# Scale arithmetic from VectorE to GpSimd, a dependency between the last two half products, and another order list

## The chip, the cores and the metric

The kernel runs on one core of a Trainium2 chip. The time is the device time in microseconds (us) of one execution, the median of several runs. The engines are PE (TensorE, matrix products, with its weight loads as PEld), DVE (VectorE), ACT (ScalarE), POOL (GpSimd) and SP, which issues the transfers here. Each engine runs its own list of instructions in order and waits on semaphores for the others.

## The reference

`x` is 4 x 8 x 512 x 64 and `state` 4 x 8 x 32 x 64. Attention goes both ways between them, its result is 2176 rows of 512, and two MLPs follow.

```
scores = scale * x @ state^T;  a = softmax(scores)  (sum + 1e-9);  xread = a @ state
scores2 = scale * state @ x^T; a2 = softmax(scores2) (sum + 1e-9); sread = a2 @ x
x = concat([xread, sread], axis=2)  -> rows of H*D = 512, 2176 of them
h = x @ w_in            (512 -> 2048)
g = h * tanh(softplus(h))
x = g @ w_out           (2048 -> 512)
xn = x / sqrt(mean(x*x) + 1e-6) * rms_g
g = xn @ w_gate; val = xn @ w_val       (512 -> 1536)
out = (g * sigmoid(g) * val) @ w_out2   (1536 -> 512)
```

## The kernel before

The rows are worked on in four chunks of 512 (one for each batch) and one of 128 rows for the state reads. A weight matrix is cut in column or row groups of 512, `wi` and `wo` of the first MLP (four groups u each), `wg`, `wv` and `w2` of the second (three each). The first products of the run are full float32 ones (`full_l1` in `full_group`, L978, and `full_l2`, L1002, on PE). Later ones take a weight or an activation as a sum of two float16 parts, high and low, and in the second MLP products of quarters are combined in the manner of Strassen (L1255 for gate and value, L1339 `lprod` for the last layer), so that DVE and ACT have sums of quarters to form.

For the float16 parts each tensor is scaled by a power of two. `pow2` (L398 to L421) finds it: PE sums norms over the partitions (L402), DVE reduces and bounds them (L410, L411 or L413), a shift leaves an exponent `q` (L414), and two integer operations on one column (or four) make of it the scale `s` (L416) and its inverse `si` (L417). `times` and `scalar` (L428 to L441, the instruction is L439) form products of such scales, and `bounds` (L873 to L886, L876, L881, L882) products, minima and maxima of them. They live in columns of small tiles named `page`. `split` (L543 to L556) then writes the scaled high part (`sh`, through `copy_to`, L385 to L392, on ACT at L388 or on DVE at L390 and L392) and the low part (`sl`, DVE, L550). `fetch` (L456 to L520) loads a weight and joins its words: `hi` (L388 or L392), `low` (L492 on ACT, L494 on DVE), `sign` (L499 or L503), and the join on DVE (L517).

`attention` (L655 to L830) has for its first heads, in DVE's and ACT's lists: a transpose of the scores (L778), their maxima (L783, L785, L786), the exponentials on ACT (L789), and for the softmax over the state a maximum, a subtraction (L791, L792) and exponentials (L794), totals (L798 to L800), a product (L803) and a transpose back (L805).

`finish` ends a chunk: the last products go to PSUM banks a_89 to a_92, DVE adds them to partial sums (`end add`, L1393), adds what was kept from an earlier pass (`end more`, L1399), and the results leave by transfers on SP's queue. For the last chunk the product A22 T4 is done in two halves, each followed by an add on DVE (L1445).

Nothing is scheduled on the chip. Every piece of work is an `op` with the engines that can take it, a cost in us (the planner's, no measurement), and the names it reads and writes. The order in which ops are emitted is a written-out list of numbers, `SEQ` (L32 to L136): a number halved is the op, and its low bit says that an op which can go to ACT or DVE takes DVE. `Plan.run` walks the list:

```
        for k in SEQ:
            o = self.ops[k >> 1]
            assert o.deps <= done
            done.add(o)
            e = "V" if k & 1 else next(x for x in o.engs if x != "V" or len(o.engs) == 1)
```

The order on each engine is that of the list; waits between engines are put in afterwards, from what the instructions read and write. A PSUM bank that one engine reads is not read by another at the same time, and it is not written while it is still read.

Of the kernel before, what the change touches and what calls it, by code (L numbers as in the profile page):

```python
# [211 lines left out]
def v1(n):  # L212
    return 0.069 + n / 960
# [23 lines left out]
def attn_moe_moe_kernel(  # L237
# [12 lines left out]
    nc = tc.nc  # L250
# [146 lines left out]
    def pow2(part, pnames, k, floor, nm, xexp, most=0, to=None):  # L397
# [10 lines left out]
        def fn(e):  # L408
            if most:
                nc.vector.tensor_reduce(t, P[b][:, :k], AX.X, ALU.max)  # L410
                nc.vector.tensor_scalar(t, t, floor, 2.0 * most, ALU.max, ALU.mult)  # L411
            else:
                nc.vector.tensor_scalar(t, P[b][:, :k], floor, 2.0, ALU.max, ALU.mult)  # L413
# [1365 lines left out]
```

## Time and profile before

| | before |
|---|---|
| median of 3 runs | 708.99 us (708.34 to 709.17) |
| the profiled execution | 707.23 us, of which the span is 705.4 |
| granted clock of PE | 0.999 of full speed |
| busy in the span | PE 691.7, DVE 645.2, ACT 435.5, POOL 0.7 us |

The span reaches from the first to the last instruction that the profiler records. Busy is the time in which an engine had an instruction in work; small instructions on DVE and ACT overlap with their neighbours, so what one of them costs its engine is the distance from its start to the next start, which can be shorter than its duration.

### The profile page before, as it was taken

The numbers are of one execution on the slowest core, as the hardware profiler recorded it, in microseconds if no ns is written. First come the engines' busy times: TensorE is split into PE (matmuls) and PEld (weight loads), VectorE is DVE, ScalarE is ACT, GpSimd is POOL, SyncE is SP. The second block draws the span as 40 slices with busy tenths as digits, with TensorE's granted clock in tenths as the row PEclk, the third lists the DMA queues.
The fourth block names the chain that finished last, engine by engine and source line by source line (L and its number), as shares of the span: only waits on it lengthen the run. The fifth ranks groups of instructions, "written<-read, shape, count | busy, mean of one in ns | idle before, by whom it ended". The sixth has DMA issues, their size and how long they took to land.

```text
span 705.4 us, 14169 instructions
## 1 busy us (share of the span) xinstructions
PE 691.7 (98%) x5818; PEld 491.2 (70%) x5818; DVE 645.2 (91%) x1182; ACT 435.5 (62%) x729; POOL 0.7 (0%) x6
## 2 busy tenths in 40 slices
PE   8899999999999999999999999999999999999996
PEld 6444444444444444476898889988889988898985
DVE  5999999999999999999999999997788687899997
ACT  5999999998896899898956565332122222123330
POOL 0000000000000000000000000000000000000000
PEclk9999999999999999999999999999999999999999
DMA  7786524256245571375810021520056630333225
GB/s 242 222 253 196 206 91 136 89 173 202 76 169 170 211 246 72 129 249 206 288 43 36 25 91 44 194 108 31 16 214 216 213 136 31 120 136 107 88 70 185
DMA packets 42100, 101.05 MB, mean 143 GB/s; under 512 B 16692, under 2 KB 18740, under 8 KB 39604
## 3 DMA queue, kind: packets, MB, share of 16 engines
q1 hardware_dynamic: 42036, 100.15, 41.9%
q8 instruction: 45, 0.74, 0.4%
q14 instruction: 19, 0.16, 0.1%
HBM read 67.90 MB, written 32.24 MB: 142 GB/s over the span
## 4 chain that ended last, share of the span: by engine, by line
PE 75%; DVE 19%; ACT 3%; DMA 2%; issue 1%; SPq 0%; DVEq 0%; ACTq 0%
PE p L1255 28%; PE a L1120 14%; PE a L1339 13%; PE p L1044 6%; PE a L1002 4%; PE p L978 2%; PE p L1486 2%; DVE g L1082 2%; PE p L1052 2%; DVE psm L550 1%; DVE slot L1137 1%; PE a L1533 1%; DVE rms L939 1%; DVE slot L1393 1%; DMA attm<-in_moe_w_gate_dram 1%
## 5 line engine op out<-in xcount | busy, mean ns | idle before, releaser
L1120 PE MATMUL a<-g,w2m 128*128 128x512 f16 (+1 forms) x864 | 164.3, 343 | 0.6 <-DVE g L1082 0.4
L1120 PEld LDWEIGHTS <-w2m 128*128 128x128 f16 x864 | 75.6, 98 | 81.3 <-issue 7.0
L1255 PEld LDWEIGHTS <-attm 128*128 128x128 f16 x1008 | 98.3, 98 | 13.2 <-issue 1.8
L1255 PEld LDWEIGHTS <-w 128*128 128x128 f16 x1008 | 98.5, 98 | 11.4
L1267 DVE TENSOR_TENSOR tt<-p,tt 128x512 f32<-128x512 f32 x120 | 81.7, 686 | 17.1 <-PE p L1255 15.1
L1044 PE MATMUL p<-slot,rms 128*128 128x512 f16 x336 | 78.0, 379 | 0.0
L1255 PE MATMUL p<-slot,w 128*128 128x256 f16 x576 | 68.8, 273 | 0.0
L1255 PE MATMUL p<-slot,attm 128*128 128x256 f16 x576 | 68.6, 273 | 0.0
L388 ACT ACTIVATE w2m<-tt 128x512 f16<-128x512 f32 x34 | 21.0, 623 | 67.2 <-DVE tt L1306 27.1
L1339 PEld LDWEIGHTS <-w2m 128*128 128x128 f16 x576 | 56.3, 98 | 8.5 <-issue 2.0
L1044 PEld LDWEIGHTS <-rms 128*128 128x128 f16 x336 | 32.3, 98 | 40.2 <-issue 2.6
L1291 ACT ACTIVATE tt<-tt,page 128x512 f32<-128x512 f32 x36 | 25.4, 714 | 45.9 <-DVE tt L1267 45.8
L1339 PE MATMUL a<-attm,w2m 128*128 128x256 f16 x384 | 45.5, 273 | 1.6 <-DVE slot L1445 1.6
L1339 PEld LDWEIGHTS <-g 128*128 128x128 f16 x432 | 42.2, 98 | 5.4 <-DVE g L1298 0.6
L1066 ACT ACTIVATE tt<-p,page 128x512 f32<-128x512 f32 x60 | 40.0, 683 | 7.3 <-DVE g L1082 5.8
L1082 DVE SCALAR_TENSOR_TENSOR g<-tt,page,g 128x1024 f16<-128x1024 f32 (+1 forms) x32 | 38.6, 1211 | 0.3
L1298 DVE TENSOR_TENSOR w2m<-tt,w2m 128x512 f16<-128x512 f32 x51 | 34.6, 685 | 2.4 <-ACT w2m L388 2.1
L550 DVE SCALAR_TENSOR_TENSOR psm<-psm,page 128x512 f16<-128x512 f32 x49 | 36.1, 742 | 0.6 <-ACT psm L388 0.2
L388 ACT ACTIVATE psm<-psm,page 128x512 f16<-128x512 f32 (+1 forms) x46 | 32.5, 717 | 6.7 <-DVE psm L550 5.2
L1339 PE MATMUL a<-attm,g 128*128 128x256 f16 x288 | 35.2, 273 | 0.3 <-DVE g L1298 0.3
L1393 DVE SCALAR_TENSOR_TENSOR rms<-a,page,rms 128x512 f32<-128x512 f32 x38 | 28.3, 746 | 7.5 <-PE a L1339 5.9
L1317 DVE TENSOR_TENSOR tt<-tt 128x512 f32<-128x512 f32 x48 | 32.7, 687 | 0.7
(248 smaller groups left out, 1214.1 us busy)
## 6 DMA issues: line engine op xcount, KB each, us to landing
psm<-in_moe_w_out_dram SPq DMA_DIRECT2D x14, 1024.0 KB, 5.0
psm<-in_moe_w_in_dram SPq DMA_DIRECT2D x8, 1024.0 KB, 5.0
psm<-in_moe_w_val_dram SPq DMA_DIRECT2D x6, 1024.0 KB, 5.7
part<-rms SPq DMA_DIRECT2D x24, 256.0 KB, 2.6
psm<-part SPq DMA_DIRECT2D x6, 1024.0 KB
kept_wv<-psm SPq DMA_DIRECT2D x9, 512.0 KB, 4.3
kept_w<-psm SPq DMA_DIRECT2D x9, 512.0 KB, 3.5
attm<-in_moe_w_gate_dram SPq DMA_DIRECT2D x4, 1024.0 KB, 5.7
```

Of the source, the lines that this page charges most:

```text
L388: nc.scalar.activation(o, i, ACTF.Copy, scale=1.0 if scale is None else scale)
L550: op({"V": v1(512) + 0.06}, lambda e: nc.vector.scalar_tensor_tensor(lo, f, s, h, ALU.mult, ALU.subtract), r=[*fn_, *hn, sname], w=ln, nam ...
L1044: nc.tensor.matmul(P[ph], P[folds[u][k]][:, a, f:f + 128], xh[:, k, b, :], start=(k, a, b) == (0, 0, 0), stop=(k, a, b) == (1, 1, 0))
L1066: op({"A": a_ps(512) + 0.1}, lambda e, sp=sp, i=i, ph=ph, ce=ce: nc.scalar.activation(P[sp][:, 512 * i:512 * i + 512], P[ph], ACTF.Mish, s ...
L1082: nc.vector.scalar_tensor_tensor(lo, x, rh, hi, ALU.mult, ALU.subtract)
L1120: nc.tensor.matmul(P[ya[d]][:, :n], part("wo", u, f, a)[:, d * 128:(d + 1) * 128], P[g[0]][:, g[1], b, i * n:(i + 1) * n], start=first and ...
L1255: nc.tensor.matmul(P[to][:, f * 256:f * 256 + 256], part(w, u, j, a)[:, k * 256 + f * 128:k * 256 + f * 128 + 128], h[:, k, b, :], start=b ...
L1267: op({"V": v1(512)}, lambda e: nc.vector.tensor_tensor(P[to], P[bank_], P[a], ALU.add), r=[bank_, a], w=[to], name=f"{w} add")
L1298: op({"V": v1(512)}, lambda e: nc.vector.tensor_tensor(P[g][:, 1, :], P[s], P[g][:, 0, :], ALU.subtract), r=[s], w=[g], name="gl")
L1317: op({"V": v1(512)}, lambda e: nc.vector.tensor_tensor(P[o], P[a], P[b], f), r=[a, b], w=[o], name="gsum")
L1339: nc.tensor.matmul(P[to][:, t * 256:t * 256 + 256], P[g][:, a, o:o + 128], part("w2", u, j, b)[:, f * 256:f * 256 + 256], start=begin and ...
L1393: op({"V": v1(512) + 0.06}, lambda e: nc.vector.scalar_tensor_tensor(o(), two(P[bank_]), osc, a(), ALU.mult, ALU.add), r=[bank_, *an, on_] ...
```

## The change

Three things are changed. The pair `s`, `si` of `pow2` becomes an op of its own on GpSimd, and so do the products of `times` and the operations of `bounds`; 89 instructions leave DVE and stand on GpSimd. `lprod` can be told to come after another op, and the second half of the last product A22 T4 is told to come after the add of its first half. And `SEQ` is another list altogether, one row longer, with another order on every engine and other choices between ACT and DVE. Line numbers of the changed kernel are 1 higher up to `pow2`, 5 higher behind it and 6 higher at the end. In all PE has the same instructions, DVE 1111 where it had 1184, ACT 630 where it had 646, and GpSimd 100 where it had 11. Of the instructions that can stand on either, ACT has 14 fewer of 512 columns and 3 fewer of 1024; DVE has them.

```
--- before.py
+++ after.py
@@ SEQ
-32 0 4 46 62 64 58 60 6 9 10 50 34 53 74 48 70 72 66 68 76 100 82 114 138 96 90 126 154 150 80 140 226 160 162 158 164
+0 2 32 48 60 6 4 62 64 66 9 10 52 55 76 160 162 50 68 70 72 74 78 98 96 80 100 158 136 166 168 194 164 228 234 230 232
...
@@ -411,12 +412,16 @@
                 nc.vector.tensor_scalar(t, t, floor, 2.0 * most, ALU.max, ALU.mult)
             else:
                 nc.vector.tensor_scalar(t, P[b][:, :k], floor, 2.0, ALU.max, ALU.mult)
             nc.vector.tensor_scalar(
                 q, t.bitcast(I32), 24, 23, ALU.logical_shift_right, ALU.logical_shift_left)
-            nc.vector.tensor_scalar(s.bitcast(I32), q, -1, (190 + xexp) << 23, ALU.mult, ALU.add)
-            nc.vector.tensor_scalar(si.bitcast(I32), q, (64 - xexp) << 23, None, ALU.add)
-        op({"V": 0.52 + (0.18 if most else 0.0)}, fn, r=[b], w=[(nm, "s")], name=f"pow2 {nm}")
+        def scales(e):
+            nc.gpsimd.tensor_scalar(s.bitcast(I32), q, -1, (190 + xexp) << 23, ALU.mult, ALU.add)
+            nc.gpsimd.tensor_scalar(si.bitcast(I32), q, (64 - xexp) << 23, None, ALU.add)
+        op({"V": 0.31 + (0.14 if most else 0.0)}, fn, r=[b], w=[(nm, "q")], name=f"pow2 {nm}")
+        op({"G": 0.4}, scales, r=[(nm, "q")], w=[(nm, "s")], name=f"pow2 {nm}")
...
-            op({"V": 0.17}, lambda e: fn(t), r=reads, w=[nm], name=str(nm))
+            op({"G": 0.2}, lambda e: fn(t), r=reads, w=[nm], name=str(nm))
...
-            nc.vector.tensor_scalar(t, a, b, c, ALU.mult, ALU.mult if c is not None else ALU.bypass)
+            nc.gpsimd.tensor_scalar(t, a, b, c, ALU.mult, ALU.mult if c is not None else ALU.bypass)
...
-            scalar(("pr", u), [128, 2], lambda t, u=u: nc.vector.tensor_tensor(
+            scalar(("pr", u), [128, 2], lambda t, u=u: nc.gpsimd.tensor_tensor(
...
-                nc.vector.tensor_tensor(t[:, 0:1], lo, sc["pr", u][:, 0:1], ALU.min)
-                nc.vector.tensor_tensor(t[:, 1:2], hi, sc["pr", u][:, 1:2], ALU.max)
+                nc.gpsimd.tensor_scalar(t[:, 0:1], lo, sc["pr", u][:, 0:1], None, ALU.min)
+                nc.gpsimd.tensor_scalar(t[:, 1:2], hi, sc["pr", u][:, 1:2], None, ALU.max)
...
-    def lprod(to, g, u, j, begin=False, ts=(0, 1)):
+    def lprod(to, g, u, j, begin=False, ts=(0, 1), after=()):
...
-        op({"T": cost}, fn, r=[g, *part_names("w2", u, [j])], w=[to] if len(ts) == 2 else [(to, ts[0])], at=clock[0],
+        op({"T": cost}, fn, r=[g, *part_names("w2", u, [j])], w=[to] if len(ts) == 2 else [(to, ts[0])], at=clock[0], after=after,
...
+            got = []
             for k in range(2):
-                lprod(B_, gs["A22"], u, T4, ts=(k,))
-                op({"V": v1(256) + 0.06}, lambda e, k=k, v=v: nc.vector.scalar_tensor_tensor(
+                lprod(B_, gs["A22"], u, T4, ts=(k,), after=got)
+                got = [op({"V": v1(256) + 0.06}, lambda e, k=k, v=v: nc.vector.scalar_tensor_tensor(
                     v[:, k], two(P[B_])[:, k], osc, two(P[a1])[:, k], ALU.mult, ALU.add),
-                    r=[(B_, k), B_, a1, on_], w=rd[k:k + 1], name="end add")
+                    r=[(B_, k), B_, a1, on_], w=rd[k:k + 1], name="end add")]
```

Three places of the order, on DVE unless another engine is named. First the start, where the heads' scores (PSUM banks a_89 to a_92, two banks for each of two halves of the heads, here called the first and the second head) become exponentials. Before, DVE has:

```order
L783 TENSOR_REDUCE page_104<-a_89 128x1 [waits PE_49]
L783 TENSOR_REDUCE page_104<-a_90 128x1 [waits PE_49]
L785 TENSOR_REDUCE page_69<-page_104 128x1 [waits DVE_49]
L786 TENSOR_SCALAR page_69<-page_69 128x1 [waits DVE_49]
L778 STREAM_TRANSPOSE attm<-a_89 128x256 [waits Activation_49]
L778 STREAM_TRANSPOSE attm<-a_90 128x256 [waits Activation_49]
L791 TENSOR_REDUCE page_104<-attm 128x16 [waits DVE_49]
L778 STREAM_TRANSPOSE attm<-a_91 128x256 [waits PE_49]
L778 STREAM_TRANSPOSE attm<-a_92 128x256 [waits PE_49]
```

After, the same place on DVE reads:

```order
L783 STREAM_TRANSPOSE attm<-a_89 128x256 [waits PE_49]
L783 STREAM_TRANSPOSE attm<-a_90 128x256 [waits PE_49]
L788 TENSOR_REDUCE page_104<-a_89 128x1
L788 TENSOR_REDUCE page_104<-a_90 128x1
L790 TENSOR_REDUCE page_69<-page_104 128x1 [waits DVE_49]
L791 TENSOR_SCALAR page_69<-page_69 128x1 [waits DVE_49]
L796 TENSOR_REDUCE page_104<-attm 128x16
L797 TENSOR_TENSOR attm<-attm,page_104 128x512 [waits DVE_49]
L788 TENSOR_REDUCE page_105<-a_91 128x1 [waits PE_49]
L788 TENSOR_REDUCE page_105<-a_92 128x1 [waits PE_49]
L790 TENSOR_REDUCE page_104<-page_105 128x1 [waits DVE_49]
L791 TENSOR_SCALAR page_104<-page_104 128x1 [waits DVE_49]
```

The next two there are the transposes of a_91 and a_92, each marked as waiting for ACT. So the transposes of the first head have moved ahead of its maxima, and those of the second behind the second head's maxima and its exponentials. On ACT the exponentials of the second head (a_91, a_92) stood behind three conversions of weights:

```order
L789 ACTIVATE attm,page_104<-a_90,page_69 128x256
L388 ACTIVATE w_70<-psm 128x1024 [waits DMAHW4_49]
L499 ACTIVATE sxm<-psm 128x1024
L492 ACTIVATE sxm<-psm 128x1024
L789 ACTIVATE attm,page_105<-a_91,page_104 128x256 [waits DVE_49,PE_49]
```

After, ACT has at that place:

```order
L794 ACTIVATE attm,page_104<-a_90,page_69 128x256
L504 ACTIVATE sxm<-psm 128x1024 [waits DMAHW4_49]
L389 ACTIVATE w_70<-psm 128x1024
L497 ACTIVATE sxm<-psm 128x1024
L497 ACTIVATE xs<-psm 128x1024 [waits DMAHW5_49]
L794 ACTIVATE attm,page_105<-a_91,page_104 128x256 [waits DVE_49,PE_49]
```

A fourth conversion, of the next transfer's words, has moved ahead of the exponentials. The second place is the first `pow2` of a weight on DVE (the scales are in page_69, q is in page_106, the weight in w_70). Before:

```order
L410 TENSOR_REDUCE page_106<-p_85 128x1 [waits PE_49]
L411 TENSOR_SCALAR page_106<-page_106 128x1 [waits DVE_49]
L414 TENSOR_SCALAR page_106<-page_106 128x1 [waits DVE_49]
L416 TENSOR_SCALAR page_69<-page_106 128x1 [waits DVE_49]
L417 TENSOR_SCALAR page_69<-page_106 128x1
L803 TENSOR_TENSOR attm<-attm,page_105 128x512
L392 TENSOR_SCALAR w_70<-w_70,page_69 128x512 [waits DVE_49]
```

After, with the pair gone to GpSimd (L420 and L421 there):

```order
L411 TENSOR_REDUCE page_106<-p_85 128x1 [waits PE_49]
L412 TENSOR_SCALAR page_106<-page_106 128x1 [waits DVE_49]
L416 TENSOR_SCALAR page_106<-page_106 128x1 [waits DVE_49]
L508 TENSOR_SCALAR sxm<-psm 128x1024 [waits DMAHW3_49]
L508 TENSOR_SCALAR xs<-psm 128x1024 [waits DMAHW4_49]
L393 TENSOR_SCALAR w_70<-w_70,page_69 128x512 [waits Pool_49]
```

Two instructions of 1024 columns now stand between q and the first use of the scale, which waits for GpSimd. The third place is the end of DVE's list (a_90 holds A22 T4, in two halves, and before that T3's product; a_91 holds first c22's product, then the last one, S4 W22). Before:

```order
L1399 TENSOR_TENSOR rms<-rms,attm 128x512 [waits DVE_49]
L1393 SCALAR_TENSOR_TENSOR rms<-a_90,page_118,rms 128x512 [waits PE_49]
L1399 TENSOR_TENSOR rms<-rms,attm 128x512 [waits DVE_49]
L1393 SCALAR_TENSOR_TENSOR slot_81<-a_91,page_118,rms 128x2x256 [waits DVE_49,PE_49]
L1399 TENSOR_TENSOR rms<-rms,attm 128x512
L1445 SCALAR_TENSOR_TENSOR slot_81<-a_90,page_118,rms 128x256 [waits DVE_49,PE_49]
L1445 SCALAR_TENSOR_TENSOR slot_81<-a_90,page_118,rms 128x256 [waits PE_49]
L1393 SCALAR_TENSOR_TENSOR slot_81<-a_91,page_118,rms 128x2x256 [waits PE_49]
```

After:

```order
L1398 SCALAR_TENSOR_TENSOR rms<-a_90,page_118,rms 128x512 [waits PE_49]
L1404 TENSOR_TENSOR rms<-rms,attm 128x512 [waits DVE_49]
L1404 TENSOR_TENSOR rms<-rms,attm 128x512
L1451 SCALAR_TENSOR_TENSOR slot_81<-a_90,page_118,rms 128x256 [waits DVE_49,PE_49]
L1398 SCALAR_TENSOR_TENSOR slot_81<-a_91,page_118,rms 128x2x256 [waits DVE_49]
L1451 SCALAR_TENSOR_TENSOR slot_81<-a_90,page_118,rms 128x256 [waits PE_49]
L1404 TENSOR_TENSOR rms<-rms,attm 128x512
L1398 SCALAR_TENSOR_TENSOR slot_81<-a_91,page_118,rms 128x2x256 [waits DVE_49,PE_49]
```

The first half's add has moved ahead of the add of c22, and one of the `end more` additions behind both halves.

## Rows read from the trace of the kernel before

**Rows 1.** The page: busy time by engine, and the chain that ended last.

```profile
PE 691.7 (98%) x5818; PEld 491.2 (70%) x5818; DVE 645.2 (91%) x1182; ACT 435.5 (62%) x729; POOL 0.7 (0%) x6
...
PE 75%; DVE 19%; ACT 3%; DMA 2%; issue 1%; SPq 0%; DVEq 0%; ACTq 0%
```

**Rows 2.** Stretches: length, busy PE, PEld, DVE, ACT, POOL; granted clock, DMA share, GB/s.

```profile
20.00:300.00 280.00, 276.35 (x1795) 127.28 (x1784) 270.92 (x545) 258.34 (x434) 0.00 (x0) 1.00 0.50 165
300.00:620.00 320.00, 319.63 (x3102) 279.55 (x3101) 283.94 (x482) 142.80 (x238) 0.00 (x0) 1.00 0.36 126
```

**Rows 3.** Timeline of DVE at small operations: start, duration, line, operation.

```profile
23.51 0.15 DVE L414 TENSOR_SCALAR page<-page 128x1 int32<-128x1 int32 x1
...
23.77 0.14 DVE L417 TENSOR_SCALAR page<-page 128x1 int32<-128x1 int32 x1
23.83 0.68 DVE L803 TENSOR_TENSOR attm<-attm,page 128x512 f32<-128x512 f32 x1
...
111.86 0.22 DVE L439 TENSOR_SCALAR page<-page 128x4 f32<-128x4 f32 x1
111.99 0.75 DVE L550 SCALAR_TENSOR_TENSOR w<-w,page 128x512 f16<-128x512 f32 x1
```

**Rows 4.** Timelines of DVE and of ACT at scalings of 512 columns.

```profile
26.68 0.48 DVE L392 TENSOR_SCALAR w<-w,page 128x512 f16<-128x512 f32 x1
27.08 0.75 DVE L503 TENSOR_SCALAR sxm<-psm 128x1024 uint16<-128x1024 uint16 x1
...
23.90 0.62 ACT L388 ACTIVATE slot<-tt 128x512 f16<-128x512 f32 x1
24.41 0.60 ACT L388 ACTIVATE attm<-a 128x512 f32<-128x512 f32 x1
```

**Rows 5.** Timeline of POOL, two of its six rows.

```profile
0.34 0.10 POOL L1764 MEMSET const-uint8-127<- 128x1 uint8 x1
...
1.01 0.29 POOL masks.py:199 TENSOR_SCALAR_AFFINE_SELECT ident<-ident 128x128 f32<-128x128 f32 x1
```

**Rows 6.** Timelines of ACT, DVE and PE in the start, up to 39 us.

```profile
10.75 1.16 ACT L388 ACTIVATE w<-psm 128x1024 f32<-128x1024 f32 x1
11.79 1.37 ACT L499 ACTIVATE sxm<-psm 128x1024 f16<-128x1024 f32 x1
13.01 1.34 ACT L492 ACTIVATE sxm<-psm 128x1024 uint16<-128x1024 uint16 x1
...
8.31 0.75 DVE L783 TENSOR_REDUCE page<-a 128x1 f32<-128x256 f32 x2 [0.89 <-PE a L739]
...
10.45 0.91 DVE L778 STREAM_TRANSPOSE attm<-a 128x256 f32<-128x256 f32 x2 [1.01 <-ACT attm L789]
...
13.11 0.67 DVE L792 TENSOR_TENSOR attm<-attm,page 128x512 f32<-128x512 f32 x1
...
14.29 0.75 DVE L783 TENSOR_REDUCE page<-a 128x1 f32<-128x256 f32 x2
...
15.33 0.68 DVE L792 TENSOR_TENSOR attm<-attm,page 128x512 f32<-128x512 f32 x1
...
38.45 4.13 PE L1002 MATMUL a<-tt,w2m 128*128 128x512 f32 x9
```

**Rows 7.** Timelines of DVE and PE in the tail.

```profile
695.16 0.68 DVE L1399 TENSOR_TENSOR rms<-rms,attm 128x512 f32<-128x512 f32 x1
695.76 0.75 DVE L1393 SCALAR_TENSOR_TENSOR rms<-a,page,rms 128x512 f32<-128x512 f32 x1
696.55 0.69 DVE L1399 TENSOR_TENSOR rms<-rms,attm 128x512 f32<-128x512 f32 x1
...
698.80 0.48 DVE L1445 SCALAR_TENSOR_TENSOR slot<-a,page,rms 128x256 f32<-128x256 f32 x1
...
701.50 0.75 DVE L1393 SCALAR_TENSOR_TENSOR slot<-a,page,rms 128x512 f32<-128x512 f32 x1 [0.83 <-PE a L1339]
...
699.33 2.12 PE L1339 MATMUL a<-attm,w2m 128*128 128x256 f16 x18 [1.65 <-DVE slot L1445]
```

205 rows, old and new, of the table SEQ are left out of this document.

## The prediction, made before the changed kernel ran

> **What bounds the kernel now.** I read the page's summary first [rows 1]. PE is busy 691.7 us of the 705.4 us span (98%), DVE 645.2 (91%), and the chain that ended last is 75% PE and 19% DVE. So PE's own work is the floor, and what a change can win is the time in which PE waits, or DVE's part of the chain. The table by stretch [rows 2] says where that can be. From 300 to 620 us PE is busy 319.63 of 320 us: nothing is to be had there. From 20 to 300 us PE, DVE and ACT are all nearly full: of 280 us PE is busy 276.35, DVE 270.92 and ACT 258.34. This is the stretch where weights are split and scaled, and nearly all of the small scale operations stand in it. DVE has 9.1 us of idle time there and PE 3.7, so a DVE that is later by 1 us is soon a PE that is later by nearly as much. From 620 us on come the last products and the tail, with one visible stall of PE.
>
> The sum below is made against the profiled execution's own 707.23 us (span 705.4 and 1.8 around it). The median of the timed runs is 708.99, 1.76 above it, and I add that back at the end. 0.2% of it is 1.4 us, about what a measurement of this kernel can tell from no change.
>
> **GpSimd: what leaves DVE.** The change takes 89 instructions from DVE: 38 scales (19 pairs), 39 products of scales, 12 of the bounds. What they cost DVE is not their duration but the start-to-start distance, since small instructions overlap. A pair [rows 3]: q (L414) starts at 23.51, the second of the pair at 23.77, the next large instruction at 23.83. Without the pair the next could start about 0.07 after q (the step from the second scale to what follows is 0.06), so a pair frees 0.32 - 0.07 = 0.25 us. A product [rows 3]: 111.86 to 111.99, 0.13 us. A bounds instruction I count like the second scale, 0.06. Sum: 19 x 0.25 + 39 x 0.13 + 12 x 0.06 = 4.8 + 5.1 + 0.7 = 10.6 us of DVE.
>
> **What the new list gives back.** DVE falls by only 73 instructions and ACT by 16: the net of the operations that may stand on either engine moves to DVE, 14 of 512 columns and 3 of 1024, with one small one the other way. On DVE a scaling of 512 columns takes 0.40 us from start to start [rows 4], and I count one of 1024 as at most two of these: 14 x 0.40 + 3 x 0.80 = 8.0. On ACT 512 columns take 0.51 [rows 4] and 1024 take 1.04 (10.75 to 11.79 in [rows 6]): 14 x 0.51 + 3 x 1.04 = 10.3. So the large item of this change is not on DVE: DVE is relieved by 10.6 - 8.0 = 2.6 us, ACT by 10.3, and ACT is not the engine of the last chain.
>
> **What the scales cost on GpSimd.** The trace of before has no GpSimd arithmetic. Its nearest rows are a memset of one column, 0.10 us, and a select on 128 columns, 0.29 us [rows 5]. The select is a real operation on data, so I take it as the upper price: 0.58 us for a pair against the 0.14 that the pair now takes. The wait is then paid only where DVE or ACT want the scale at once. In the new order DVE has other work between q and the first use nearly everywhere (at the first pair two instructions of 1024 columns, as the rows of the order show); by my count of the list only two or three of the 19 have less than 0.6 us of cover. I take +0.4 us in all; without any cover it would be 19 x (0.58 - 0.25) = 6.3. A rule speaks against this move. The Trainium skill, "SBUF — State Buffer", section "Who interferes with whom", says that DVE and GpSimd share a pair of ports as an exclusive lock: a DVE instruction with two SBUF inputs, or in a two-port mode, and a GpSimd instruction that reads SBUF block one another for a whole instruction. No row here shows it, as GpSimd does nothing after 1.3 us. What a hold would cost is worked out among the rivals.
>
> **The start.** The new list orders the first attention heads differently. Before [rows 6]: DVE reduces the first head's maxima at 8.31, waits 1.01 us for ACT's exponentials of that head and transposes at 10.45; ACT converts weights from 10.75 on. After: DVE transposes first (0.91 us for the two, as the row at 10.45), so it takes the maxima from 9.2 to 10.3 (1.04 us, as the second head's from 14.29 to 15.33 [rows 6]), and ACT's first exponentials run from about 10.4 to 11.3. Then ACT does four conversions of weights, one more than before, ahead of the second head: 11.3 + 1.04 + 3 x 1.22 (10.75 to 11.79, and 11.79 to 13.01 for each of the others [rows 6]) = 16.0, and only then this head's exponentials, the first of them done at about 16.6. DVE's transposes of the second head now stand behind these (the list shows the wait for ACT). DVE reaches that place at about 12.5: 10.3, then 1.18 for a subtraction and a reduction (13.11 to 14.29 [rows 6]) and 1.04 for the second head's maxima. So it idles some 4.1 us where it idled 1.01: +3.1. From there to the join of the first second-layer weight (L517) the new list has 0.9 us less of DVE work, added up by such distances. The join ends about 2.1 us later, and with it PE's first product with that weight, L1002, which now starts at 38.45 [rows 6], just behind the join. Term: **+2.1**. If PE could be held by something else there, it is 0; if the list saves nothing, 3.1.
>
> **The middle.** Of DVE's relief of 2.6 us, 0.9 was used up in the start; 1.7 is left, nearly all before 300 us, where DVE has little idle time. ACT's 10.3 us can shorten only DVE's and PE's waits for ACT. PE has 3.7 us of idle time in the stretch [rows 2], a part of it first-use waits which no order removes. I take the 1.7 us and a little for ACT, 2.3 in all: **-2.3**. The bounds are 0 (PE's later waits are for other things) and -5.8: all of the 3.7 us and the 2.1 us of the start made good.
>
> **The tail.** PE does the first half of A22 T4, then its second half, then S4 W22. Before [rows 7]: the last adds on DVE run in the order u3, more, c22, more, half; the half's add starts at 698.80, and PE, done with the first half at 699.33 - 1.65 = 697.68, waits 1.65 us for it. Already now PE waits there, since it shares the bank, so the new "after" tells only the plan of a wait that exists. What changes is DVE's order: u3, more, more, half, c22, half, more, c12. The half's add can then start at 695.76 + 0.79 + 2 x 0.60 = 697.75 (distances of these rows), about when PE is done, in place of 698.80. PE starts its second half about 1.0 us earlier. c22's add, which S4 W22 needs (same bank), now comes right behind and ends at about 699.0, as the second half does. The last add (701.50 before) comes at about 700.5: **-1.0**. Bounds 0 and -1.65.
>
> **Sum.** +0.4 + 2.1 - 2.3 - 1.0 = -0.8 us: 706.4 for the profiled execution, 708.2 for the median.
>
> **The rivals.**
> (a) ACT's relief is worth more than I give it. For: in 20 to 300 us ACT is busy 92%, so it and DVE wait for each other in turn; then the start's delay and PE's idle time are made good. Against: DVE is fuller than ACT there, and its net relief is small. With the middle at its bound of -5.8, the sum is -4.3: 704.7.
> (b) GpSimd holds DVE. If each of the 89 instructions stopped DVE for 0.1 us (the memset's duration), that is 8.9 us on the engine which sets the pace to 300 us, and the sum is +8.1: 717.1; at 0.05 us each, +3.7: 712.7. DVE's net relief of 2.6 us is gone at 0.029 us each, and the forecast's gain of 0.8 at 0.009. For: DVE is busy 97% there, so almost any GpSimd instruction meets one on DVE. Against: the operations are of 1 to 4 columns, and even the 128 columns of the select took 0.29 us from end to end. By the Trainium skill's page "SBUF — State Buffer" a meeting costs up to a whole instruction of either engine.
> (c) The start's delay stays and the middle gives nothing, as PE's waits there are for first uses: +0.4 + 2.1 - 1.0 = +1.5, 710.5. Unless the middle gives at least 1.5 us, the kernel is not faster.
> (d) Nothing shows: terms of 1 to 2 us cancel and the time is within 0.2%. This is the forecast's own neighbourhood.
>
> **How the numbers follow.** Forecast, which (d) belongs to (706.7 to 709.7): 0.44; (a) 0.27; (b) 0.14; (c) 0.15. The forecast's -0.8 lies inside the 1.4 us, so of its 0.44 I give 0.16 to faster and 0.28 to same; (a) is faster but for 0.01; (c) is split, 0.03 same and 0.12 slower; (b) is slower. Faster 0.42, same 0.32, slower 0.26. The range runs from beyond (a), 703.5 (its middle, and the tail too, near their bounds), to (b) at 0.05 us each, 712.7; outside lie the stronger forms of (b) and of (a), 0.2 together.
>
> **What the new profile would show.** GpSimd: 89 more instructions, a few tenths each, and DVE's large instructions no longer than now (a hold would show as longer 512-column rows in the stretch to 300). DVE busy less by well under 11 us, ACT by about 10. DVE idle for some 4 us from about 12.5, PE's first L1002 near 40.5. PE's wait between the last halves 0.6 us or so. PE's busy share in 300 to 620 us unchanged. I would be wrong if L1002's first row starts by 39, if the DVE rows grow, or if waits for GpSimd appear with more than 1 us in sum.

## The result, and the profile of the changed kernel

The changed kernel takes 718.76 us (median of 4 runs, 717.43 to 719.38) against 708.66 for the one before on the same chip: ratio 1.0144, interval 1.0121 to 1.0166. It is 10 us slower; the forecast was 708.2 with a range to 712.7. The profiled execution took 719.38 us, with a span of 717.6, 12.2 above the one before.

The page of the changed kernel, busy time by engine [rows 1]:

```profile
PE 699.2 (97%) x5818; PEld 493.6 (69%) x5818; DVE 647.6 (90%) x1109; ACT 425.9 (59%) x713; POOL 52.2 (7%) x95
```

DVE has 73 instructions fewer and is busy 2.4 us longer; ACT is relieved by 9.6. GpSimd, with 89 small instructions more, is busy 51.6 us with them. What PE waits for, longest first (line, releaser, total, times, longest):

```profile
PE a L1125 <- ACT slot L389: 6.0, 1, 6.0
PE p L958 <- DVE w L522: 3.7, 2, 2.9
PE p L932 <- ACT tt L1071: 1.2, 1, 1.2
...
PE a L1344 <- DVE slot L1451: 0.6, 1, 0.6
```

Two stretches of the table, in the columns of [rows 2], first of the kernel before and then of the changed kernel (PE's granted clock stands behind the count of POOL: 1.00 twice before, 0.83 and 0.91 after):

```profile
20.00:40.00 20.00, 17.92 (x162) 9.83 (x151) 19.66 (x45) 19.62 (x39) 0.00 (x0) 1.00 0.78 237
120.00:160.00 40.00, 39.69 (x321) 18.09 (x319) 39.05 (x85) 39.01 (x66) 0.00 (x0) 1.00 0.40 126
...
20.00:40.00 20.00, 17.96 (x136) 10.33 (x137) 18.27 (x35) 15.77 (x33) 1.74 (x2) 0.83 0.70 207
120.00:160.00 40.00, 33.99 (x220) 13.91 (x219) 32.66 (x56) 34.03 (x59) 4.76 (x15) 0.91 0.29 93
```

Two waits stand out, one near 21 us and one near 125 us. To place the 12.2 us I took the distance from each of PE's matmuls to the next, less the median distance for that shape in the same run, and added these up by stretch, before and after: up to 60 us 14.0 and 18.7 us (+4.6), from 60 to 120 us 3.6 and 2.6 (-1.0), from 120 to 160 us 4.4 and 11.6 (+7.2), from 160 to 340 us 9.2 and 12.5 (+3.3, in small pieces), from 340 to 690 us 1.9 and 0.9 (-1.0), in the tail 1.8 and 0.8 (-1.0). The sum is 12.1.

The wait near 125 us, followed back. PE and ACT first:

```profile
127.16 6.16 PE L1125 MATMUL a<-g,w2m 128*128 128x512 f16 x18 [6.01 <-ACT slot L389]
...
139.24 4.06 PE L1125 MATMUL a<-g,w2m 128*128 128x512 f16 x18
...
123.18 1.15 ACT L389 ACTIVATE g<-tt,page 128x1024 f16<-128x1024 f32 x1 [6.96 <-POOL page L444]
...
126.43 1.84 ACT L389 ACTIVATE slot<-a,page 128x512 f32<-128x512 f32 x3
```

PE waits for a copy by ACT that frees its banks, ACT waits 6.96 us for a scale (`page`, L444) from GpSimd. The same 18 matmuls take 6.16 us behind the wait and 4.06 us at 139 us, 2.1 us more. The table by stretch shows why: from 125 to 131 us the granted clock is 0.50, the lower of the two levels (1.2 GHz in place of 2.4).

```profile
125.00:131.00 6.00, 3.84 (x10) 1.32 (x10) 5.59 (x10) 5.94 (x13) 0.00 (x0) 0.50 0.65 203
```

It is part of the price of a long wait. GpSimd in that time:

```profile
110.54 0.62 POOL L420 TENSOR_SCALAR page<-page 128x1 int32<-128x1 int32 x1 [2.06 <-DVE page L416]
111.22 0.47 POOL L421 TENSOR_SCALAR page<-page 128x1 int32<-128x1 int32 x1
...
113.79 3.07 POOL L886 TENSOR_SCALAR page<-page 128x1 f32<-128x1 f32 x1
116.83 0.55 POOL L887 TENSOR_SCALAR page<-page 128x1 f32<-128x1 f32 x1
...
119.18 1.50 POOL L444 TENSOR_SCALAR page<-page,page 128x4 f32<-128x4 f32 x4
...
121.82 1.06 POOL L444 TENSOR_SCALAR page<-page,page 128x4 f32<-128x4 f32 x4
122.85 0.30 POOL L444 TENSOR_SCALAR page<-page 128x4 f32<-128x4 f32 x1
```

A run of 22 instructions lasts from 110.54 to 123.15. Near its end they take some 0.3 us each; before that up to 3.07. ACT was ready for the scale at 116.22 (123.18 less its wait). Had each of the 22 taken the 0.30 us that such an instruction takes alone (e5 below), the run would have ended near 117.1, an estimate. By it the order made the wait possible, and the slow pace ahead of the scale made most of it. DVE beside the longest one:

```profile
113.64 1.28 DVE L1087 SCALAR_TENSOR_TENSOR g<-tt,page,g 128x1024 f16<-128x1024 f32 x1
114.84 0.75 DVE L555 SCALAR_TENSOR_TENSOR w<-w,page 128x512 f16<-128x512 f32 x1
115.50 1.29 DVE L522 SCALAR_TENSOR_TENSOR psm<-psm,sxm 128x512 int32<-128x512 int32 x2
116.83 0.49 DVE L393 TENSOR_SCALAR psm<-psm,page 128x512 f32<-128x512 f32 x1
...
124.37 1.28 DVE L1087 SCALAR_TENSOR_TENSOR g<-tt,page,g 128x1024 f16<-128x1024 f32 x1 [4.57 <-ACT g L389]
```

GpSimd's minimum of one column stands for 3.07 us, as long as DVE runs four instructions with two tensors in SBUF back to back, and ends as DVE begins one with a single tensor (116.83). This is the rule that the prediction held against the change: in the Trainium skill, "SBUF — State Buffer", sections "Who interferes with whom" and "Summary: rules for kernel authors", the later one of the two is blocked for the whole instruction of the other. The trace agrees in part: GpSimd came second (113.79 behind 113.64) and was blocked, but it stood through three more DVE instructions that began after it. DVE's rows did not grow: the 281 additions of two tensors of 512 columns in f32 took 0.685 us in the mean before and 0.686 after.

The start [rows 6], DVE and PE:

```profile
16.69 0.90 DVE L783 STREAM_TRANSPOSE attm<-a 128x256 f32<-128x256 f32 x2 [3.80 <-ACT attm L794]
...
29.18 0.16 DVE L411 TENSOR_REDUCE page<-p 128x1 f32<-128x2 f32 x1 [1.30 <-PE p L403]
...
41.88 1.23 DVE L522 SCALAR_TENSOR_TENSOR w2m<-w2m,sxm 128x1024 int32<-128x1024 int32 x1
...
21.14 1.06 PE L958 MATMUL p<-w,attm 64*32 64x512 f32 x8 [2.85 <-DVE w L522]
...
43.16 3.70 PE L1007 MATMUL a<-tt,w2m 128*128 128x512 f32 x8
```

DVE idles 3.80 us up to 16.69 as foreseen; PE's first second-layer product starts at 43.16, 4.7 us later than before, not 2.1. The tail [rows 7]:

```profile
710.98 0.48 DVE L1451 SCALAR_TENSOR_TENSOR slot<-a,page,rms 128x256 f32<-128x256 f32 x1
...
711.51 2.13 PE L1344 MATMUL a<-attm,w2m 128*128 128x256 f16 x18 [0.63 <-DVE slot L1451]
```

PE's wait between the halves is 0.63 us where it was 1.65.

### The profile page after: what moved, and what is told of

Its sections match the earlier page's. It is cut to its first block, busy times and chain, and to the rows that moved or that the text cites. A ratio compares the mean times of both kernels' runs of the same rounds, so it can differ in the third digit from the quotient of the medians.

```text
span 717.6 us, 14175 instructions
## 1 busy us (share of the span) xinstructions
PE 699.2 (97%) x5818; PEld 493.6 (69%) x5818; DVE 647.6 (90%) x1109; ACT 425.9 (59%) x713; POOL 52.2 (7%) x95
## 4 chain that ended last, share of the span: by engine, by line
PE 46%; DVE 10%; ACT 2%; issue 1%; POOL 0%; DVEq 0%
PE p L1260 29%; PE a L1344 13%; PE p L1492 2%; DVE psm L555 1%; PE a L1539 1%; DVE g L1087 1%; DVE slot L1232 1%; DVE rms L1166 1%; DVE slot L1398 1%; PE a L1125 1%; DVE rms L1223 1%; PE p L1171 0%; DVE tt L1272 0%; DVE attm L555 0%; DVE psm L522 0%
## 5 line engine op out<-in xcount | busy, mean ns | idle before, releaser
L1260 PEld LDWEIGHTS <-attm 128*128 128x128 f16 x1008 | 98.4, 98 | 11.6
L1272 DVE TENSOR_TENSOR tt<-p,tt 128x512 f32<-128x512 f32 x120 | 81.0, 686 | 12.5 <-PE p L1260 6.1
L389 ACT ACTIVATE tt<-p 128x512 f32<-128x512 f32 x33 | 19.2, 594 | 36.5 <-PE p L1260 29.0
L420 POOL TENSOR_SCALAR page<-page 128x1 int32<-128x1 int32 (+1 forms) x19 | 11.5, 603 | 399.3 <-DVE page L416 399.2
```

Source lines behind the costliest of these rows:

```text
L389: nc.scalar.activation(o, i, ACTF.Copy, scale=1.0 if scale is None else scale)
L1260: nc.tensor.matmul(P[to][:, f * 256:f * 256 + 256], part(w, u, j, a)[:, k * 256 + f * 128:k * 256 + f * 128 + 128], h[:, k, b, :], start=b ...
L1272: op({"V": v1(512)}, lambda e: nc.vector.tensor_tensor(P[to], P[bank_], P[a], ALU.add), r=[bank_, a], w=[to], name=f"{w} add")
```

## The experiments

Ratios are to the kernel before, run on the same chip beside each. "Early" means that each GpSimd operation stands right behind its inputs in the list. Edits of the list are shown by its effect on an engine's rows.

| kernel | median us | ratio (interval) |
|---|---|---|
| changed kernel | 718.76 | 1.0144 (1.0121 to 1.0166) |
| e1 new list, all on DVE | 725.25 | 1.0249 (1.0230 to 1.0269) |
| e14 the same, early | 724.76 | 1.0238 (1.0208 to 1.0269) |
| e3 new list, pairs alone on GpSimd | 723.82 | 1.0230 (1.0211 to 1.0250) |
| e2 old list, all 89 on GpSimd | 706.63 | 0.9984 (0.9969 to 0.9998) |
| e4 changed kernel, old start | 716.83 | 1.0134 (1.0114 to 1.0154) |
| e6 kernel before, new start | 712.85 | 1.0055 (1.0029 to 1.0080) |
| e10 changed kernel, two products moved | 717.93 | 1.0139 (1.0114 to 1.0164) |
| e11 the same and old start | 715.46 | 1.0105 (1.0080 to 1.0130) |
| e15 changed kernel, early | 711.77 | 1.0049 (1.0031 to 1.0067) |
| e16 the same and old start | 709.41 | 1.0014 (1.0001 to 1.0026) |
| e17 as e15, two exponentials moved | 707.15 | 0.9989 (0.9978 to 1.0001) |
| e9 as e15, old choices of engine | 773.44 | 1.0929 (1.0910 to 1.0948) |
| e8 kernel before, new tail | 708.42 | 1.0005 (0.9991 to 1.0019) |
| e13 old list, GpSimd early, new tail | 707.69 | 0.9990 (0.9976 to 1.0003) |

**List against engine.** e1 takes the operations back to DVE in the changed kernel, e2 gives them to GpSimd in the kernel before, e3 takes back all but the pairs.

```diff
 e1 (in the changed kernel; e3 leaves the two lines of the pair)
-            nc.gpsimd.tensor_scalar(s.bitcast(I32), q, -1, (190 + xexp) << 23, ALU.mult, ALU.add)
+            nc.vector.tensor_scalar(s.bitcast(I32), q, -1, (190 + xexp) << 23, ALU.mult, ALU.add)
...
-            nc.gpsimd.tensor_scalar(t, a, b, c, ALU.mult, ALU.mult if c is not None else ALU.bypass)
+            nc.vector.tensor_scalar(t, a, b, c, ALU.mult, ALU.mult if c is not None else ALU.bypass)
 e2 (in the kernel before): the same lines the other way round
```

> The new list and the new tail, with all 89 scale operations issued on DVE again, each at the place where the list has it. Three theories. Chain: the scales of the products and bounds, nineteen of them in a row on GpSimd, come late for ACT's scaled copies, and that is most of the loss (PE's wait of 6 us at 127 us of the changed kernel); then the wait is gone, DVE has 10.6 us more work of which a part is given back, and the time is 711 to 714. Hold: GpSimd stops DVE's instructions, some 0.05 us each; then about 4 us come back, less than DVE's work grows by, and the time stays near 717 to 720. List: the new order itself is slower and GpSimd has nothing to do with it; 717 to 720, with PE's wait at about 127 us still there.

> The list and the tail of before, with all 89 operations on GpSimd. Chain: the scales come late at the same two groups of bounds (about 105 and 112 us of before), so ACT waits there and PE after it; 2 to 8 us slower, 711 to 717, in one or two visible waits. Hold: 3 to 5 us slower, 711 to 714, spread over the stretch to 300 us with no single wait. List: not slower than before, 706 to 709.

> The new list and tail with only the 19 pairs of scales on GpSimd; products and bounds are back on DVE. Chain: the wait at 127 us is gone, and the start's delay stays; 711 to 713. Hold: 38 of 89 instructions are left, so a little over half of GpSimd's part comes back; 714 to 716. List: 717 to 720.

All three came out against the theory that I held, the chain (scales late on GpSimd make the loss), and against the hold; e1 and e3 also lie above the 717 to 720 that I gave for the list. With all on DVE the new list is slower still (1.0249), and with the old list GpSimd costs nothing (0.9984). So GpSimd by itself is not the loss; it comes only with the new list, and that list needs GpSimd. The page of e2 says how much DVE is relieved in the old list, that of e1 how much in the new one:

```profile
PE 692.0 (98%) x5818; PEld 491.6 (70%) x5818; DVE 638.2 (90%) x1093; ACT 435.1 (62%) x729; POOL 48.1 (7%) x95
...
PE 699.0 (97%) x5818; PEld 492.1 (68%) x5818; DVE 656.3 (91%) x1198; ACT 425.8 (59%) x713; POOL 0.7 (0%) x6
```

In the old list 645.2 - 638.2 = 7.0 us, in the new one 656.3 - 647.6 = 8.7. The new list gives DVE back 647.6 - 638.2 = 9.4 us with GpSimd, and 656.3 - 645.2 = 11.1 without.

e1 had a flaw: its operations stood where the list has GpSimd do them, which is late for DVE (ACT waited 3.4 us for a product at 88 us). e14 puts them right behind their inputs:

> The new list with all small operations on DVE, as in the first experiment, but each placed right behind its inputs and not where the list has GpSimd do it. If the first one's 725 came from scales that stood too late on DVE (ACT waited 3.4 us for one at 88 us): 715 to 720. If it came from DVE's work (8 us more than before from the operations that moved from ACT): 722 to 726.

It changes nothing (1.0238), so the places are not the reason. DVE's load is left as the likely one; e15 below bears it out.

**The start.** e4 takes the order of before up to PE's first L1007 into the changed kernel, and with it the choice between ACT and DVE of four operations; e6 takes the new start into the kernel before; on DVE the rows are those of the change section, in both directions.

```diff
 e4, DVE
-L783 STREAM_TRANSPOSE attm<-a_89 128x256
-L783 STREAM_TRANSPOSE attm<-a_90 128x256
 L788 TENSOR_REDUCE page_104<-a_89 128x1
 ...
+L783 STREAM_TRANSPOSE attm<-a_89 128x256
+L783 STREAM_TRANSPOSE attm<-a_90 128x256
 ...
```

> The changed kernel with the start of the old list: everything up to PE's first product of the second layer is in the order of before, the rest in that of the new list; all 89 operations on GpSimd. Chain: PE's wait of 6 us stays, only the start's 4.6 us come back, less what the middle had made good; 714 to 716. List, in the form that the start is what matters and the later wait follows from it: 709 to 711 and no wait at about 127 us. Hold: 714 to 716 too, with no change of the rows behind the start.

> The kernel before (all on DVE) with only the start taken from the new list, up to PE's first product of the second layer. If the start's order by itself costs time: 3 to 5 us slower, 710.5 to 712.5, with DVE idle for 4 us from about 12.6 us and PE waiting at 21 us. If the rest of the old list makes it good: within 1.5 us of before.

The new start by itself costs 0.55%, 3.9 us (e6). In the changed kernel its removal gave 0.1% of the time, within the intervals, and PE's wait of 6.0 us stayed, ahead of the same product.

**GpSimd's queue.** In the new list two scales that ACT needs at 116 and 118 us stand behind a run of bounds and products whose users come much later. e10 moves the first of them and its input; e15 puts every GpSimd operation right behind its inputs, which moves both. In neither does an instruction of another engine move.

```diff
 e10, POOL
+L444 TENSOR_SCALAR page_107<-page_69 128x4
+L444 TENSOR_SCALAR page_107<-page_107 128x4
 L420 TENSOR_SCALAR page_69<-page_106 128x1
 L421 TENSOR_SCALAR page_69<-page_106 128x1
 L881 TENSOR_TENSOR page_107<-page_69 128x2
 ...
-L444 TENSOR_SCALAR page_107<-page_69 128x4
 ...
-L444 TENSOR_SCALAR page_107<-page_107 128x4
```

> The changed kernel with two of GpSimd's instructions moved: the two products behind the scale that ACT waits for at 123 us stand in front of the run of some twenty bounds and products of later groups, not behind it. No instruction of PE, DVE or ACT moves. Queue theory: ACT's wait of 7 us, DVE's of 4.6 and PE's of 6 go, with the low clock behind it; 6 to 8 us faster than the changed kernel, 710 to 713. List theory: GpSimd's queue only covers waits that the new order has anyway; at most 2 us come back, 716 to 719.

> The same two moved, and the start in the order of before as well. If the two losses are separate they add: 3 to 4 us below the kernel with only the two moved, 707 to 709, so about the time of before. If the start's loss is made good later (start restored alone brought 0.1% on the clock of the runs, 3.6 us in the trace), 710 to 713, as with the two moved alone.

> The changed kernel with each of GpSimd's operations placed right behind its inputs; PE's, DVE's and ACT's own orders are untouched. In the changed kernel two scales that ACT needs at 116 and 118 us stand behind a run of bounds and products for later groups; with the first of them moved, ACT stopped at the second (5.4 us). Queue theory: with both out of the way PE's wait of 6 us near 125 us is gone; 6 to 8 us faster than the changed kernel, 710.5 to 713. List theory: the wait moves to the next thing again; 715 to 718.

> The same, with the start in the order of before as well. The two losses taken as separate: 3 to 4 us below the one before, 707 to 709, equal to before within its uncertainty. If a third of about 3 us is hidden in the rest of the new list (the stretch from 220 to 340 us, where the changed kernel waits 2 us more): 709.5 to 711.5.

e10 alone looked like a refutation. ACT's timeline in it shows why it was none: the copy that had waited runs at 116.12, and the next one with a scale from the same run takes the wait over.

```profile
116.12 1.15 ACT L389 ACTIVATE g<-tt,page 128x1024 f16<-128x1024 f32 x1
...
124.91 1.84 ACT L389 ACTIVATE slot<-a,page 128x512 f32<-128x512 f32 x3 [5.38 <-POOL page L444]
```

In e15 that copy runs at 118.78, PE has no wait there, and 7 us are back (1.0144 to 1.0049), though GpSimd's run is no shorter (109.78 to 124.54).

```profile
118.78 1.83 ACT L389 ACTIVATE slot<-a,page 128x512 f32<-128x512 f32 x3
```

PE's waits in e15 begin with the start's:

```profile
PE p L958 <- DVE w L522: 3.3, 2, 2.8
PE p L932 <- ACT tt L1071: 1.1, 1, 1.1
```

With the old start as well (e16) 1.0014 is left.

e14 and e15 have the same list and differ only in the engine of the 89 operations: 1.0238 and 1.0049, so in this list and in order of need GpSimd is worth 13 us. DVE's busy time differs by 10.8:

```profile
PE 701.2 (97%) x5818; PEld 493.2 (68%) x5818; DVE 657.7 (91%) x1198; ACT 426.6 (59%) x713; POOL 0.7 (0%) x6
...
PE 696.8 (98%) x5818; PEld 492.6 (69%) x5818; DVE 646.9 (91%) x1109; ACT 425.7 (60%) x713; POOL 58.0 (8%) x95
```

**Which part of the start.** e17 moves two instructions of ACT in e15 and nothing else.

```diff
 e17, ACT
 L504 ACTIVATE sxm<-psm 128x1024
+L794 ACTIVATE attm,page_105<-a_91,page_104 128x256
+L794 ACTIVATE attm,page_105<-a_92,page_104 128x256
 L389 ACTIVATE w_70<-psm 128x1024
 L497 ACTIVATE sxm<-psm 128x1024
 L497 ACTIVATE xs<-psm 128x1024
-L794 ACTIVATE attm,page_105<-a_91,page_104 128x256
-L794 ACTIVATE attm,page_105<-a_92,page_104 128x256
```

> The changed kernel with GpSimd's operations in order of need (711.8, ratio 1.0049) and with only ACT's two exponentials of the second head moved, from behind four conversions of weights to behind the first one; DVE's and PE's orders are untouched. If they are what makes the start late: DVE's idle time of 3.8 us near 13 us shrinks to 1 us or less, the joins and PE's L958 come 2 to 3 us earlier, ratio 1.001 to 1.003. If the conversions, now later by 0.9 us, and the rest of the new order hold the joins anyway: less than 1 us, ratio 1.004 to 1.006.

It gave 0.6%, 4.2 us, more than I expected of it and more than the whole old start (e16). Its DVE and PE rows:

```profile
13.46 0.91 DVE L783 STREAM_TRANSPOSE attm<-a 128x256 f32<-128x256 f32 x2 [0.70 <-ACT attm L794]
...
38.30 3.70 PE L1007 MATMUL a<-tt,w2m 128*128 128x512 f32 x8
```

The two exponentials were the whole of the start's loss: DVE's idle time goes from 3.80 to 0.70 us, L1007 is at 38.30, where it was at 38.45 before the change, and the granted clock from 20 to 40 us is 1.00 again. At 0.9989 this is the new list with its two faults mended, level with the kernel before; its median is 0.8 us lower, and the interval just reaches 1. The old list with the same operations on GpSimd does as well (e2, 0.9984), so nothing here shows a gain from the new order.

**Choices of engine.** e9 keeps e15's order and takes the choice between ACT and DVE from before for each operation (162 of them differ).

```diff
 the list, low bit of an entry: 1 takes DVE
-... 328 285 521 181 522 214 525 526
+... 328 285 521 180 522 214 525 526
```

> The new order on PE and of the list, GpSimd's operations in order of need, but with the choice between ACT and DVE of before for each operation: DVE has some 8 us less to do, ACT some 10 more. If DVE is what holds the stretch to 300 us: 2 to 5 us faster than with the new choices, ratio 0.998 to 1.002. If order and choices were fitted to one another: slower, ratio 1.006 to 1.012, with waits for ACT.

773 us: the order is fitted to its choices, and neither can be judged without the other. PE waits most for norms on ACT, in the same columns as above:

```profile
PE p L403 <- ACT junk L542: 11.5, 5, 4.5
```

It says nothing on whether the moves from ACT to DVE are good in a list made for them.

**The tail.** e8 is the kernel before with the last adds in the new order; e13 adds GpSimd, early.

```diff
 e8, DVE
-L1399 TENSOR_TENSOR rms<-rms,attm 128x512
 L1393 SCALAR_TENSOR_TENSOR rms<-a_90,page_118,rms 128x512
-L1399 TENSOR_TENSOR rms<-rms,attm 128x512
+L1399 TENSOR_TENSOR rms<-rms,attm 128x512 x2
+L1445 SCALAR_TENSOR_TENSOR slot_81<-a_90,page_118,rms 128x256
 ...
```

> The kernel before with only the new order of the last adds on DVE. By the prediction 1.0 us less (ratio 0.9986), PE's wait between the halves 0.6 us in place of 1.65. If the last transfers or adds take it back: no change (0.9995 to 1.0005) although PE's wait shrinks.

> The old list with GpSimd's operations, each right behind its inputs, and the new order of the last adds. If the tail is worth its 1.0 us of PE's wait and GpSimd's relief about the 0.2% measured with the old list: 0.25 to 0.4% below before, 705.5 to 707. If the tail's gain is lost in the last adds and transfers: as the old list with GpSimd, 0 to 0.2% below.

PE's wait is down to 0.60 us in e8 and the last add starts 4.9 us after the start of PE's last 36 matmuls, where it was 5.9. But there is no gain (1.0005). The last rows of e8:

```profile
700.56 2.13 PE L1339 MATMUL a<-attm,w2m 128*128 128x256 f16 x18 [0.60 <-DVE slot L1445]
...
702.73 0.75 DVE L1393 SCALAR_TENSOR_TENSOR slot<-a,page,rms 128x512 f32<-128x512 f32 x1 [0.23 <-PE a L1339]
```

From 702.73 to the end of the span of 707.6 are 4.9 us, in the kernel before 3.9 (701.50 to 705.4): the output's last transfer lands 0.9 us later behind its add. The same 4.9 stands in e13, but 3.9 to 4.0 in all kernels with the new list. The trace points to the transfer ahead of it: SP issues the last two 0.7 us apart in e8 and e13 (702.81 and 703.51 in e8), 1.6 apart in the kernel before (700.70 and 702.27) and 1.3 in the changed one, so the two overlap more. No run tested it.

**GpSimd beside DVE.** e5 adds, behind the end of the kernel before, chains of 16 GpSimd multiplications of 4 columns alone and beside 16 DVE instructions of 512 columns, and these without GpSimd.

```diff
+                if pool:
+                    nc.gpsimd.tensor_scalar(gp[:, 0:4], gp[:, 0:4], 1.0, None, ALU.mult)
+                if work:
+                    work(i)
```

> The kernel before with stretches added behind its end: chains of 16 small GpSimd multiplications (4 columns, each on the last one's result) alone, and beside 16 DVE additions of two SBUF tensors of 512 columns, beside 16 DVE scalings of one, and beside 16 additions of PSUM and SBUF; each of the DVE sets also without GpSimd. What the changed kernel's trace says: alone 0.25 to 0.3 us each. If DVE's instructions with two SBUF inputs keep GpSimd out while they run: the chain beside them takes as long as they do, some 10 us in place of 4.5, and beside PSUM inputs it keeps its pace; DVE's instructions grow by under 0.1 us. If GpSimd holds DVE: the DVE additions take 0.85 us or more each. If it is only GpSimd's own unsteady speed: the same pace in all stretches.

GpSimd alone, beside additions of two SBUF tensors, beside scalings of one, and beside additions of PSUM and SBUF; then DVE's sets, each without and with GpSimd:

```profile
703.53 4.76 POOL L1756 TENSOR_SCALAR attm<-attm 128x4 f32<-128x4 f32 x16
719.15 9.25 POOL L1756 TENSOR_SCALAR attm<-attm 128x4 f32<-128x4 f32 x16
735.03 7.33 POOL L1756 TENSOR_SCALAR attm<-attm 128x4 f32<-128x4 f32 x16
752.59 4.76 POOL L1756 TENSOR_SCALAR attm<-attm 128x4 f32<-128x4 f32 x16
...
708.40 9.71 DVE L1743 TENSOR_TENSOR psm<-psm 128x512 f32<-128x512 f32 x16
718.31 9.72 DVE L1743 TENSOR_TENSOR psm<-psm 128x512 f32<-128x512 f32 x16
728.52 5.45 DVE L1746 TENSOR_SCALAR psm<-psm 128x512 f32<-128x512 f32 x16
734.16 5.45 DVE L1746 TENSOR_SCALAR psm<-psm 128x512 f32<-128x512 f32 x16
```

0.30 us each alone and beside PSUM inputs. Beside two SBUF tensors each GpSimd instruction ends some 0.08 us behind the end of a DVE addition (719.67 behind 719.59, 720.28 behind 720.20, and so on), one for each, and its chain ends when DVE's does; beside single scalings of f32 it is held back too, 0.67 us from start to start or one for two scalings. DVE's sets take the same time with and without GpSimd. Why the minimum of 3.07 us stood through four DVE instructions and not through one is not shown.

## Why the prediction was wrong

- **What the scales cost on GpSimd, +0.4: the step that failed.** It counted the cover between q and the first use of a pair and left out the 51 products and bounds, which stand in the same queue. There a scale can be late for what is ahead of it on GpSimd, whatever its own cover. The wait came at a product, with 22 instructions in a row, and cost 0.95% (e15 against the changed kernel), some 7 us with the low clock behind it. ACT's 6.96 us alone are past the 1 us of waits for GpSimd that the prediction named as a sign of being wrong. The price was off too: the select's 0.29 us was taken as the upper end, and the first and second of a pair took 0.60 and 0.51 on average; by e5, where one alone takes 0.30, because DVE keeps GpSimd out.
- **The start, +2.1: right in its mechanism, off by a factor of two.** The idle time was foreseen (4.1 us, measured 3.80) and is the whole loss (e17). The step from there to the join was wrong: I let 0.9 us of DVE's work be saved on the way, but from the first head's first row (8.31 before, 8.72 now) to the start of the join it is 27.9 us in both kernels, waits left out, and the join came 4.7 us later. PE waited 2.85 us for the first layer's join, ran the stretch from 20 to 40 us at 0.83 of its clock, and DVE then waited for PE (1.30 us at 29.18). e17 and e6 put the price at 4.2 and 3.9 us.
- **DVE's relief, 2.6 us: wrong in sign.** By busy time 7.0 us (old list, e2) or 8.7 (new list, e1) left it, not 10.6, and 9.4 or 11.1 came back, not 8.0: 2.4 us more in either reckoning. In order of need 10.8 leave it (e14 and e15), so the price of what leaves depends on the places; the price of what comes back was too low in all.
- **The middle, -2.3: not there.** With the two faults mended (e17) PE's lost time between 60 and 690 us is 19.6 us against 19.0 before. ACT's relief of 9.6 us shows as no gain there, as the prediction's own reason against rival (a) had it.
- **The tail, -1.0: right in the trace** (0.63 us for 1.65) in the changed kernel; in the kernel before it gave no time (e8).
- **Rivals.** (b), GpSimd holds DVE: no hold shows. In the changed kernel a scaling of 512 columns to f16 does take longer to the next start with GpSimd at work (a median of 0.52 us) than without (0.40), but that comes from what follows it: where the low part of the same tile comes next, which reads its result, the median is 0.52 us in 11 cases of the kernel before, with GpSimd idle, and 0.52 in the changed kernel both with GpSimd at work (12) and without (15). Compared by shape and by what follows, the 63 places with GpSimd at work that have like ones without are 0.8 us longer in sum. In the old list the move cost nothing (e2), and e5 shows DVE unhindered: the lock worked the other way round. (c), the start's delay stays and the middle gives nothing, came true and was the smaller half. The case that held most, an urgent scale behind others that are not, was among none of them. The range ended at 712.7 since (b) was priced at 0.05 us for each instruction and no queue was priced at all.

What stays open: why the last transfer lands later with the new tail in the old list, where the one ahead of it is a suspicion and no more; the 3 us in small pieces from 160 to 340 us, of which no single wait was tested; and why the old start as a whole gives less than e17 (0.35% in e16, 0.1% in e4; PE's lost time up to 60 us, reckoned as above, is 16.4 us in e16 and 13.6 in e17).

## What to carry to other kernels

When small operations move to an idle engine, list that engine's queue in order with the first user of each result: an urgent result comes no earlier than all that stands ahead of it, at its real price beside the other engines, has been done. A queue in order of need can be worth as much as the move itself: some 7 us here, where the move out of order gave 7 us in the new list (e1 against the changed kernel) and 1 us in the old one (e2). When one wait in such a run is removed, look at what the next consumer waits for before the theory is given up. And an order list and its engine choices are one object: test a new list by mending it, one or two rows at a time, not by exchanging a part of its assumptions.

## What was not expected of the hardware

In the changed kernel GpSimd's instructions of 1 to 4 columns took from 0.19 to 3.07 us. A chain of them took 0.30 us each alone and beside DVE instructions that read PSUM, 0.58 beside DVE additions of two SBUF tensors (9.25 / 16), where it advanced by one with the end of each, and it was slowed by f32 scalings of one SBUF tensor as well (7.33 us, 2.8 of it after they had ended), while DVE's time was the same to 0.01 us in 9.7. And a wait of 6 us on PE cost 2.1 us more behind it: 18 matmuls at 6.16 us in place of 4.06, with a granted clock of 0.50 from 125 to 131 us.
